# A recorded order of work for a two-layer linear-attention kernel, with its first loads on one queue and more zero matmuls

## The chip, the cores and the metric

The kernel runs on one core of a Trainium2 chip. Five engines work side by side, each through its own list of instructions in order: TensorE (PE: matmuls, with its weight loads shown as PEld), VectorE (DVE), ScalarE (ACT), GpSimd (POOL) and SyncE (SP), which here only issues DMAs. An instruction that waits holds up all that stand behind it on its engine. The metric is the device time of one execution in microseconds (us). A profiled execution gives the trace; its span runs from the first to the last instruction.

## What is computed

The reference applies four residual blocks to `x` of 2048 rows by 512 columns in bfloat16: attention, gated unit, attention, gated unit. Both attentions share one set of weights, and both gated units another.

```python
x = x + _A_ref(_layernorm(x), wqkv, w_phi, wo)            # attention, 32 heads of 16
x = x + _B_ref(_layernorm(x), W_gate, W_up, W_down)       # gated unit, 1376 wide
x = x + _A_ref(_layernorm(x), wqkv, w_phi, wo)
x = x + _B_ref(_layernorm(x), W_gate, W_up, W_down)

def _A_ref(x, wqkv, w_phi, wo):
    q, k, v = split(x @ wqkv)                             # by head
    pq, pk = q @ w_phi, k @ w_phi                         # per head, 16 by 16
    phi_q = concat(softmax(pq), softmax(-pq))             # 32 features per head
    phi_k = concat(softmax(pk), softmax(-pk))
    kv, z = sum_s(phi_k * v), sum_s(phi_k)                # over all 2048 rows
    o = (phi_q @ kv) / (phi_q @ z + 1e-6)
    return o @ wo

def _B_ref(x, W_gate, W_up, W_down):
    gate = x @ W_gate
    return ((gate * (gate > 0)) * (x @ W_up)) @ W_down
```

Because `kv` and `z` are sums over all rows, no row can be attended before the keys of every row are done. This is the one barrier in each layer.

## The kernel before, in words

The rows are cut into 16 tiles of 128 rows, and four tiles make a chunk. `X` stays in the on-chip memory from the first load to the last store; the weights are loaded once.

**Start** (`setup`, `feature_weights`). The projection to keys and `w_phi` are folded into one matrix `Wk2`: TensorE transposes the key weights (L351, 16 matmuls), ACT or DVE copies them out of PSUM (L307, L309), TensorE multiplies by the block matrix `Wblk` that DVE makes of `w_phi` (L327, L364), and ACT casts the result (L307). `Wq2` for the queries is made later in the same way, with DMA transposes (L337). The loads are issued at L225 to L240: the key weights, tiles 1 to 3 of `X` and the value weights on SP; tile 0, `w_phi`, the other tiles and the query weights on ACT. `wake` (L318) multiplies zeros by zeros three times on TensorE, results unused.

**Each layer.** `Norm` takes mean and variance by DVE (L388, L390), the power of minus one half on POOL (L398), scales on ACT (L460) or DVE (L472), and transposes the tile by DMA (L486 for two tiles, L490 for one) or by TensorE (L481). `keys_values` multiplies by `Wk2` (L710), takes both exponentials on ACT (L715), sums them on DVE (L682, or L692 and L688 with a first addition on POOL at L679), inverts (L724), scales on POOL and DVE (L730), multiplies for the values (L663) and adds each tile into `kv` on TensorE (L752). `build_R` turns `kv` into the block matrix `R` (L774, DVE). `queries` does for the queries what was done for the keys (L794, L798, L803, L807, L814), ending in a DMA transpose on SP (L816). `attention` multiplies by `R` (L833), divides (L851, L853), transposes, projects with `wo` (L884) and adds to `X` (L566). `Centre` prepares the gated unit's input (L524, L527, L548, transposes at L535, L539, L542). `glu` runs per chunk, in parts of one to four tiles (`PARTS`): the last 96 columns (L593 to L603), ten gate and ten up products (L613), ReLU and product (L619 to L630), and the down products (L645), added to `X` at L570 or L566. In the second layer, each finished tile goes out by a DMA of SP (L650).

**What sets the order.** No engine's list is written out. Every operation is entered in a `Plan` with an engine, an assumed duration, what it reads and writes, and its buffers. `Plan.order` then plays the program through by these durations: at each moment it takes, for each free engine, the ready operation with the highest rank, which is the length of the chain behind it plus an offset from the table `RANK` for its group and tile. It also picks which of a kind's buffers an operation gets. `emit` writes the operations out in the order so found. `WF_IN` to `X_IN` are the assumed arrival times of the first loads, `LOADED` the time from which the other weights may be loaded. `STEP` chooses, tile by tile, which engine does an operation, how a transpose is done, and how many zero matmuls there are.

Of the kernel before, what the change touches and what calls it, by code (L numbers as in the profile page):

```python
# [8 lines left out]
P = 128  # L9
D = 512  # L10
# [3 lines left out]
NDB = D // P  # L14
# [14 lines left out]
BF16 = mybir.dt.bfloat16  # L29
F32 = mybir.dt.float32  # L30
# [20 lines left out]
TAIL = {"PE": 0.165, "ACT": 0.12, "DVE": 0.115, "POOL": 0.045, "SP": 0.0}  # L51
SAME = {"PE": -0.165, "ACT": 0.035, "DVE": 0.035, "POOL": 0.08, "SP": 0.0}
HOPS = {("DVE", "POOL"): 0.09, ("ACT", "POOL"): 0.15}
NEXT = {"PE": 0.055, "SP": 0.03}
FREE = 0.06


def hop(a, b):
    return SAME[a] if a == b else HOPS.get((a, b), NEXT.get(b, 0.04))


class Plan:
# [10 lines left out]
    def op(self, eng, occ, fn, reads=(), writes=(), holds=(), lat=0.0, at=0.0, group=None, port=False, long=False):  # L73

        o = Op()
        o.eng, o.occ, o.cost, o.fn, o.lat, o.at, o.port, o.long = eng, occ, occ + TAIL[eng], fn, lat, at, port, long
        o.group, o.i_in = group or self.group
        base, slope = RANK.get(f"{o.group}.{eng}") or RANK[o.group]
        o.bias = base - slope * o.i_in
        o.preds, o.succs, o.i = set(), [], len(self.ops)  # L80
        for k in reads:
            w, rs = self.state.setdefault(k, (None, []))
# [16 lines left out]
    def order(self):  # L99
        for o in self.ops:  # L100
            for p in o.preds:
                p.succs.append(o)
        for o in reversed(self.ops):
            o.rank = o.cost + o.lat + max([s.rank + hop(o.eng, s.eng) for s in o.succs], default=0.0)
        free = {k: [0.0] * n for k, (pool, n) in self.kinds.items()}
        engines = sorted({o.eng for o in self.ops})
        busy = {e: 0.0 for e in engines}
        ready = {e: [] for e in engines}
        for o in self.ops:
            o.wait, o.t0 = len(o.preds), o.at  # L110
            if not o.wait:
                ready[o.eng].append(o)
        seq, left, now, shut = [], len(self.ops), 0.0, 0.0
        while left:
            moved, later = False, []
            for e in engines:
                if busy[e] > now + 1e-9:
                    later.append(busy[e])
                    continue
                best = None  # L120
                for o in ready[e]:
                    if o.t0 > now + 1e-9:
                        later.append(o.t0)
                        continue
                    if o.port and shut > now + 1e-9:
                        later.append(shut)
                        continue
                    ok = True
                    need = {}
                    for b in o.bufs:  # L130
                        if b.slot is None:
                            need[b.kind] = need.get(b.kind, 0) + 1
                    for k, n in need.items():
                        got = [t for t in free[k] if t is not None]
                        if len(got) < n:
                            ok = False
                        else:
                            t = sorted(got)[n - 1]
                            if t > now + 1e-9:
                                later.append(t)  # L140
                                ok = False
                    if ok and (best is None or (o.rank + o.bias, -o.i) > (best.rank + best.bias, -best.i)):
                        best = o
                if best is None:
                    continue
                o = best
                ready[e].remove(o)
                moved, left = True, left - 1
                o.start, end = now, now + o.cost
                busy[e] = now + o.occ  # L150
                if o.long:
                    shut = end
                later.append(busy[e])
                for b in o.bufs:
                    if b.slot is None:
                        b.slot = min((i for i, t in enumerate(free[b.kind]) if t is not None),
                                     key=lambda i: free[b.kind][i])
                        free[b.kind][b.slot] = None
                        b.end = 0.0
                    b.left -= 1  # L160
                    b.end = max(b.end, end + o.lat + FREE)
                    if not b.left:
                        free[b.kind][b.slot] = b.end
                for s in o.succs:
                    s.wait -= 1
                    s.t0 = max(s.t0, end + o.lat + hop(e, s.eng))
                    if not s.wait:
                        ready[s.eng].append(s)
                seq.append(o)
            if not moved:  # L170
                later = [t for t in later if t > now + 1e-9]
                assert later, "the plan is stuck"
                now = min(later)
        self.seq = seq
        return seq
# [833 lines left out]
```

## Time and profile before

| | before |
|---|---|
| runs, median (lowest to highest) | 382.15 us (380.12 to 382.57), three runs |
| profiled execution, its own time | 380.91 us |
| its span | 379.2 us |
| TensorE busy | 363.6 us, 96% of the span |
| DVE, ACT, POOL busy | 268.0, 205.5, 121.1 us |
| moved by DMA | 32.61 MB, 8.44 MB of it read from HBM |

The profiled execution took 1.71 us more than its span, and stands 1.24 us below the median of the runs. Busy shares are means over stages with different limits, so they are read stage by stage below. A row of the timeline gives the start, the duration, the engine, the line, the operation, what it writes and reads, how many follow each other, and in brackets the idle time before it with what ended it. The rows of a table by windows give, for a stretch of the span, its length and the busy time of each engine in it.

### The profile page before, as it was taken

How to read it: one execution, taken by the hardware profiler on the slowest of the kernel's cores; microseconds unless marked ns; L12 is line 12 of the kernel's file. 1: busy time of each engine (PE TensorE's matmuls, PEld its weight loads, DVE VectorE, ACT ScalarE, POOL GpSimd, SP SyncE). 2: the span in 40 equal slices, each digit the busy share in tenths (PEclk: the TensorE clock that was granted, in tenths of full speed). 3: DMA queues.
4: the chain of work that ended last, by engine and by line, in shares of the span. 5: the costliest groups of instructions: out<-in, count | busy, mean ns of one | idle time of the engine just before them, and what ended most of it. 6: DMA issues, size and time to landing. Idle time of an engine off the chain costs nothing.

```text
span 379.2 us, 6724 instructions
## 1 busy us (share of the span) xinstructions
PE 363.6 (96%) x2380; PEld 189.9 (50%) x2409; DVE 268.0 (71%) x608; ACT 205.5 (54%) x439; POOL 121.1 (32%) x203
## 2 busy tenths in 40 slices
PE   4898999999899999999999999999999999999996
PEld 2444545756445444444444456475654445454444
DVE  4999999999925442763497998999962675172433
ACT  4898979776762446737706925865234135514100
POOL 3798965131110220560155681724310002000000
PEclk9999999999999999999999999999999999999999
DMA  8889936788950230021013070478930075000011
GB/s 262 239 143 227 260 44 144 133 149 146 145 107 2 42 58 15 0 30 27 0 22 77 9 119 3 87 127 146 171 85 14 5 146 115 14 0 16 1 55 57
DMA packets 98882, 32.61 MB, mean 86 GB/s; under 512 B 90560, under 2 KB 98336, under 8 KB 98848
## 3 DMA queue, kind: packets, MB, share of 16 engines
q1 hardware_dynamic: 97216, 29.93, 39.7%
q10 hardware_dynamic: 1632, 2.24, 1.8%
q8 instruction: 19, 0.31, 0.4%
q14 instruction: 15, 0.12, 0.1%
HBM read 8.44 MB, written 2.10 MB: 28 GB/s over the span
## 4 chain that ended last, share of the span: by engine, by line
PE 64%; DVE 24%; DMA 6%; issue 2%; ACT 1%; POOL 1%; SPq 0%; POOLq 0%; ACTq 0%
PE ps L613 37%; PE ps L645 14%; PE ps L884 5%; DMA b<-b 4%; DVE sk L682 4%; DVE rk L724 3%; DVE bnst L388 3%; PE ps L794 3%; PE ps L593 3%; DVE sk L692 2%; DVE b L730 2%; PE q L833 2%; DMA X<-in_A_x_dram 2%; DVE sq L682 1%; DVE sk L688 1%
## 5 line engine op out<-in xcount | busy, mean ns | idle before, releaser
L613 PE MATMUL ps<-b,wu 128*128 128x512 bf16 (+2 forms) x400 | 79.2, 336 | 0.6 <-DMA b<-b 0.6
L613 PE MATMUL ps<-b,wg 128*128 128x512 bf16 (+2 forms) x400 | 78.6, 336 | 0.0
L645 PE MATMUL ps<-wd,b 128*128 128x512 bf16 (+3 forms) x368 | 78.1, 366 | 0.3
L623 ACT ACTIVATE b<-ps 128x512 bf16<-128x512 f32 (+2 forms) x100 | 50.5, 520 | 39.6 <-PE ps L613 39.1
L626 DVE SCALAR_TENSOR_TENSOR b<-ps,b 128x512 bf16<-128x512 f32 (+2 forms) x60 | 35.1, 598 | 39.9 <-PE ps L613 38.9
L645 PEld LDWEIGHTS <-b 128*128 128x128 bf16 (+1 forms) x374 | 35.3, 98 | 39.1
L613 PEld LDWEIGHTS <-wg 128*128 128x128 bf16 x400 | 36.1, 98 | 33.1
L613 PEld LDWEIGHTS <-wu 128*128 128x128 bf16 x400 | 36.2, 98 | 32.7 <-issue 0.9
L730 POOL TENSOR_TENSOR b<-b,rk 128x1024 bf16<-128x1024 bf16 (+6 forms) x28 | 37.5, 1351 | 9.6 <-DVE rk L724 7.9
L798 ACT ACTIVATE b<-ps 128x512 bf16<-128x512 f32 x64 | 33.0, 638 | 5.7 <-PE ps L794 5.1
L715 ACT ACTIVATE b<-ps 128x512 bf16<-128x512 f32 x64 | 33.7, 628 | 1.3 <-PE ps L710 1.3
L679 POOL TENSOR_TENSOR b<-b 128x256 f32<-128x256 bf16 x30 | 19.7, 670 | 43.9 <-ACT b L715 34.1
L570 DVE SCALAR_TENSOR_TENSOR X<-ps,r,X 128x512 bf16<-128x512 f32 (+2 forms) x26 | 18.2, 701 | 20.2 <-PE ps L645 20.1
L710 PE MATMUL ps<-Wk,b 128*128 128x512 bf16 x123 | 29.4, 379 | 2.0 <-DMA b<-b 1.2
L884 PE MATMUL ps<-wo,b 128*128 128x512 bf16 x118 | 29.7, 379 | 1.5 <-DMA b<-b 0.9
L630 DVE TENSOR_TENSOR b<-b,b 128x512 bf16<-128x512 bf16 (+2 forms) x40 | 13.5, 348 | 24.0 <-ACT b L623 22.3
L552 POOL TENSOR_SCALAR ve<-tot 128x4 f32<-128x4 f32 x8 | 1.9, 233 | 88.8 <-ACT sq L548 88.8
L663 PE MATMUL ps<-wkv,b 128*128 128x512 bf16 x122 | 29.9, 386 | 0.3
L794 PE MATMUL ps<-Wq,b 128*128 128x512 bf16 x126 | 29.5, 379 | 0.1
L548 ACT ACTIVATE sq<-b 128x512 bf16<-128x512 bf16 x32 | 20.1, 627 | 17.4 <-DVE b L527 17.0
L598 ACT CAST ur<-ps 128x192 bf16<-128x192 f32 (+1 forms) x18 | 5.4, 302 | 32.2 <-PE ps L593 32.1
L814 POOL TENSOR_TENSOR b<-b,rq 128x512 bf16<-128x512 bf16 x19 | 20.2, 1061 | 8.4 <-DVE rq L807 6.1
(94 smaller groups left out, 493.7 us busy)
## 6 DMA issues: line engine op xcount, KB each, us to landing
out_dram<-X SPq DMA_DIRECT2D x15, 128.0 KB, 1.8
X<-in_A_x_dram ACTq DMA_DIRECT2D x3, 512.0 KB, 7.2
b<-b SPq DMA_TRANSPOSE x94, 3.2
wg<-in_B_W_gate_dram SPq DMA_DIRECT2D x8, 160.0 KB, 3.2
wu<-in_B_W_up_dram SPq DMA_DIRECT2D x8, 160.0 KB, 4.0
wd<-in_B_W_down_dram SPq DMA_DIRECT2D x5, 256.0 KB, 4.7
wkv<-in_A_wqkv_dram SPq DMA_DIRECT2D x2, 512.0 KB, 7.1
wq<-in_A_wqkv_dram ACTq DMA_DIRECT2D x1, 512.0 KB, 8.3
```

Source lines behind the costliest of these rows:

```text
L613: nc.tensor.matmul(ps[:], lhsT=wt[:, b, f * P:(f + 1) * P], rhs=xnT[:, lo:hi, b, :], start=(b == 0), stop=(b == NDB - 1))
L623: pl.op("ACT", 0.045 + 0.43 * share, lambda ups=ups, ru=ru, sign=1.0 if fuse else -1.0: nc.scalar.activation(out=ru[:], in_=ups[:], func=A ...
L626: pl.op("DVE", 0.06 + 0.548 * share, lambda gps=gps, ru=ru, h=h, cs=cs: nc.vector.scalar_tensor_tensor(out=h[:, cs], in0=gps[:], scalar=0. ...
L645: nc.tensor.matmul(yps[:], lhsT=hs[f][:fsz, ti * P:(ti + 1) * P], rhs=st.wd[:fsz, f, cols], start=(f == 0), stop=(f == NFT - 1))
L663: nc.tensor.matmul(vp[:], lhsT=xnT[:, ti, kb, :], rhs=st.wkv[:, kb, D:2 * D], start=(kb == 0), stop=(kb == NDB - 1))
L710: nc.tensor.matmul(ps[:], lhsT=xnT[:, ti, kb, :], rhs=w(kb), start=(kb == 0), stop=(kb == NDB - 1))
L715: pl.op("ACT", 0.48, lambda s=s, ek=ek, pk=pk: nc.scalar.activation(out=ek[:, :, s, :], in_=pk[:].rearrange("p (j x) -> p j x", j=8), func ...
L730: eng.tensor_tensor(out=phiK[:, lo:hi, :, :].rearrange("p j s (f h) -> p (j s) f h", h=4), in0=ek[:, lo:hi, :, :].rearrange("p j s (f h) - ...
L794: nc.tensor.matmul(pq[:], lhsT=xnT[:, ti, kb, :], rhs=st.Wq2[:, kb, :], start=(kb == 0), stop=(kb == NDB - 1))
L798: pl.op("ACT", 0.48, lambda s=s, eq=eq, pq=pq: nc.scalar.activation(out=eq[:, :, s, :], in_=pq[:].rearrange("p (j x) -> p j x", j=8), func ...
L814: (nc.vector if on_dve else nc.gpsimd).tensor_tensor(out=e, in0=e, in1=rq[:].unsqueeze(2).to_broadcast([P, 8, DH, 4]), op=Alu.mult)
L884: nc.tensor.matmul(yps[:], lhsT=turned(b), rhs=st.wo[:, b, :], start=(b == 0), stop=(b == NDB - 1))
```

## The change: a recorded order, another row of loads, 26 zero matmuls

- `Plan.order` no longer plays anything through. It takes the operations in the order of a table, `ORDER`, of 1867 numbers, and gives each buffer the free slot that was used longest ago. `RANK` and the assumed gaps between engines go.
- The first loads all stand on SP, in one row: tile 0, tile 1, key weights, tiles 2 and 3, value weights, tiles 4 to 7, 8 to 11, query weights, tiles 12 to 15. Only `w_phi` is issued by ACT.
- `wake` enters 26 zero matmuls; `ORDER` says where each stands.
- `STEP` has other choices of engines, of paired transposes, and of parts (`part0` "3111", first chunk in parts of one, one and two tiles, in place of "4111", one and three). `sA` is 0: ahead of the second layer no chunk takes its mean and variance from sums gathered on the way (`add_sums`, L412); all use L388.
- A second way to compute the keys (`raw`) is entered but not used, as `raw` is 0. The assumed durations only document the table now: they no longer act.

```diff
     def order(self):
-        for o in self.ops:
-            for p in o.preds:
-                p.succs.append(o)
...
-                    if ok and (best is None or (o.rank + o.bias, -o.i) > (best.rank + best.bias, -best.i)):
-                        best = o
...
+        owner = {k: [None] * n for k, (pool, n) in self.kinds.items()}
+        last = {k: [-1] * n for k, (pool, n) in self.kinds.items()}
+        assert sorted(ORDER) == list(range(len(self.ops)))
+        self.seq = [self.ops[i] for i in ORDER]
+        for at, o in enumerate(self.seq):
+            o.place = at
+            assert all(hasattr(p, "place") for p in o.preds), "an operation before what it needs"
+            for b in o.bufs:
+                if b.slot is None:
+                    free = [i for i, u in enumerate(owner[b.kind]) if u is None or not u.left]
+                    b.slot = min(free, key=lambda i: last[b.kind][i])
+                    owner[b.kind][b.slot] = b
+            for b in o.bufs:
+                b.left -= 1
+                last[b.kind][b.slot] = at
+        return self.seq
...
+LOAD_SP = ((0, 1), (1, 2), "k", (2, 4), "v", (4, 8), (8, 12), "q", (12, 16))
+LOAD_ACT = ("f",)
...
-    nc.sync.dma_start(out=wkv[:, :, 0:D], in_=wv[:, :, D:2 * D])
-    nc.scalar.dma_start(out=X[:, 0:1, :], in_=xv[:, 0:1, :])
-    nc.scalar.dma_start(out=wf[:], in_=A_w_phi.rearrange("(b j) d f -> (j d) b f", b=NDB, j=8))
-    nc.sync.dma_start(out=X[:, 1:2, :], in_=xv[:, 1:2, :])
-    nc.sync.dma_start(out=X[:, 2:4, :], in_=xv[:, 2:4, :])
-    nc.sync.dma_start(out=wkv[:, :, D:2 * D], in_=wv[:, :, 2 * D:3 * D])
...
+    for what in LOAD_SP:
+        load(nc.sync, what)
+    for what in LOAD_ACT:
+        load(nc.scalar, what)
...
-    nc.scalar.dma_start(out=X[:, 4:8, :], in_=xv[:, 4:8, :])
-    nc.scalar.dma_start(out=X[:, 8:12, :], in_=xv[:, 8:12, :])
-    nc.scalar.dma_start(out=wq[:], in_=wv[:, :, 0:D])
-    nc.scalar.dma_start(out=X[:, 12:16, :], in_=xv[:, 12:16, :])
...
-    "part0": "4111", "part1": "6111", "tB0": "D---", "tB1": "--DA", "tA": "----", "wev": "ADADAAAAADDAAAAA",
-    "xn1": "ADAADDAPDAADDAAA", "turn": "A-AA", "wake": 3, "fuse0": "AFAA", "fuse1": "FFFF", "gate": 1, "sA": 2,
...
+    "raw": 0, "kev": "ADAD", "part0": "3111", "part1": "6111", "tB0": "DA--", "tB1": "-D-A", "tA": "----",
+    "wev": "ADAAAAAADDDAAAAA", "xn1": "ADADDAADDAADAAAA", "turn": "-A--", "wake": 26, "fuse0": "AFAA",
+    "fuse1": "FFFF", "gate": 1, "sA": 0, "xB0": "DAAAADADADDDDDAD", "xB1": "AAAAAAAADDAAAADA",
...
+ORDER = [int(i) for i in """
+142 127 0 1 126 145 132 8 149 9 2 4 3 5 10 11 12 150 133 139 141 125 140 135 138 129 151 155 159 163 131 143 6 156
...
+1866
+""".split()]
```

Counted in the two built programs, the changed one has 23 more zero matmuls of 512 columns and 4 more transposes by matmul on TensorE; 80 gate and up matmuls of 384 columns become 80 of 256 and 80 of 128. The table also moves most operations: in front of the last attention matmul (L833) of the first layer stood 160 gate and up matmuls (L613) and none of the second layer's keys or queries; in the changed order 340 stand there, with 8 of the second layer's key and 8 of its query matmuls.

157 lines of the change are left out of this document (46 added, 111 removed), and 102 rows, old and new, of tables (ORDER, RANK, STEP).

## The prediction, written before the changed kernel ran

> **What bounds the kernel now.** First the page: span and engines. Then a table by windows cut where the work changes: the start, the first layer's keys, its attention, the middle, the second layer's queries and attention, the last gated unit, the end.
>
> ```profile
> span 379.2 us, 6724 instructions
> PE 363.6 (96%) x2380; PEld 189.9 (50%) x2409; DVE 268.0 (71%) x608; ACT 205.5 (54%) x439; POOL 121.1 (32%) x203
> ...
> 0.00:14.00 14.00, 8.17 (x47) 4.77 (x48) 9.18 (x32) 7.47 (x13) 5.78 (x23) 1.00 0.89 281
> 14.00:57.00 43.00, 40.44 (x306) 20.52 (x309) 43.00 (x88) 38.68 (x76) 36.76 (x48) 1.00 0.75 168
> 57.00:100.00 43.00, 42.05 (x390) 26.40 (x395) 42.48 (x120) 31.67 (x84) 11.91 (x19) 1.00 0.79 147
> 100.00:220.00 120.00, 118.52 (x574) 55.59 (x582) 71.89 (x151) 69.66 (x142) 38.40 (x73) 1.00 0.20 37
> 220.00:280.00 60.00, 58.31 (x554) 35.70 (x558) 56.09 (x138) 31.50 (x76) 24.89 (x37) 1.00 0.59 101
> 280.00:360.00 80.00, 79.79 (x420) 38.52 (x423) 39.16 (x75) 26.52 (x53) 3.38 (x5) 1.00 0.21 45
> 360.00:379.20 19.20, 16.27 (x97) 8.44 (x95) 6.17 (x10) 0.00 (x0) 0.00 (x0) 0.99 0.17 56
> ```
>
> TensorE is the bound: after its length each row has TensorE's busy time, and what is missing to the length is all that a reordering can win. That is 5.83 us before 14 us, then 2.56, 0.95, 1.48, 1.69 and 0.21, and 2.93 at the end: 15.65 in all. From 14 to 57 us DVE is busy without a break (43.00 of 43.00), so there two engines are at their limits. The timeline of TensorE shows that the start costs more than its gaps:
>
> ```profile
> 1.24 1.46 PE L318 MATMUL ps<-zero 128*128 128x512 bf16 x3 [1.24 <-DVE zero L234]
> 5.37 1.89 PE L351 MATMUL ps<-ident,wkv 128*128 128x128 bf16 x16 [2.66 <-DMA wkv<-in_A_wqkv_dram]
> 10.04 0.61 PE L364 MATMUL ps<-Wblk,b 128*128 128x128 bf16 x4 [1.93 <-DVE b L309]
> 12.00 1.80 PE L663 MATMUL ps<-wkv,b 128*128 128x512 bf16 x4
> 13.63 1.89 PE L710 MATMUL ps<-Wk,b 128*128 128x512 bf16 x7
> ...
> 66.93 0.67 PE ps L613 x12
> 80.46 1.95 PE ps L613 x12
> 244.22 0.86 PE ps L794 x4
> ```
>
> The last three rows are from the chain that ended last, in order of time. There, four matmuls of 512 columns take 0.86 us, 0.216 each; 128 columns take 0.056 and 384 columns 0.163. At 12.00 four of 512 took 1.80 (about 0.43 each), so TensorE ran at half pace until about 13.6, after 3.6 us of unbroken work from 10.04. The granted clock reads 1.00 throughout and does not show it.
>
> **Part 1, the loads.** Landings from the page, the waits for them, and the bytes by window:
>
> ```profile
> X<-in_A_x_dram ACTq DMA_DIRECT2D x3, 512.0 KB, 7.2
> wkv<-in_A_wqkv_dram SPq DMA_DIRECT2D x2, 512.0 KB, 7.1
> X<-in_A_x_dram SPq DMA_DIRECT2D x1, 256.0 KB, 6.4
> ...
> 6.13 0.42 DVE L327 TENSOR_TENSOR Wblk<-M,wf 128x256 bf16<-128x256 bf16 x1 [1.32 <-DMA wf<-in_A_w_phi_dram]
> 8.25 0.69 DVE L388 BATCH_NORM_STATS2 bnst<-X 128x6 f32<-128x512 bf16 x1 [0.68 <-DMA X<-in_A_x_dram]
> ...
> 0.00:4.00 4.00, 1.46 (x3) 0.29 (x3) 1.18 (x8) 1.49 (x2) 1.32 (x11) 1.00 0.46 116
> 4.00:8.00 4.00, 2.63 (x24) 2.40 (x24) 2.25 (x7) 1.34 (x3) 1.10 (x4) 1.00 1.07 376
> 8.00:12.00 4.00, 2.07 (x17) 1.32 (x15) 3.75 (x12) 2.81 (x6) 2.41 (x7) 1.00 1.08 364
> ```
>
> The last number of a window is GB/s: 0.46 MB are moved by 4 us, 1.97 by 8, 3.42 by 12. The whole set is no smaller afterwards, so its last piece lands when it does now. What changes is who is served first. If one row is served in its order at these rates and a landing follows its last byte by about 0.6 us (my estimate), the key weights (0.79 MB with tiles 0 and 1 ahead) land at 5.5, against TensorE's start on them at 5.37 now; tiles 2 and 3 (1.05 MB) at 6.2 instead of 8.24; the value weights (1.57) at 7.6; tiles 4 to 7 (2.1) at 9.0. `w_phi` no longer has tile 0 ahead of it on ACT, and DVE's wait for it until 6.13 shrinks.
>
> The Trainium skill, "DMA: Bandwidth & Descriptors", section "Issuing engines are not separate DMA queues", says that DMAs of all issuing engines interleave on the same sixteen DMA engines, and that spreading them saves issue time only. By it the order alone can pay, not the number of queues; the unchanged total above agrees.
>
> **Part 2, the first keys.** In the changed order 13 zero matmuls stand ahead of the transposes of the key weights. Starting at 1.24, with 3.6 us at half pace, eight take until 4.8 and five more, at 0.216, until 5.9. That is 0.4 past the landing. The 16 transposes then take 0.9 and end at 6.8 (5.37 plus 1.89 now). ACT afterwards has three copies, a copy of tile 1's transpose and four casts, all in a row:
>
> ```profile
> L307 ACT COPY b<-ps 128x512 bf16<-128x512 bf16 x6 | 3.3, 592 | 2.8 <-PE ps L351 2.8
> L307 ACT CAST Wk<-ps 128x512 bf16<-128x512 f32 x4 | 2.3, 587 | 1.8 <-PE ps L364 1.8
> ```
>
> Four at 0.55 and four at 0.58 are 4.5; from 6.2 (the first four transposes done) this ends at 10.7. The first key matmul follows at about 10.8, at full pace. Now it comes at 13.2, behind the slow value matmuls of 12.00. **Worth 2.4 us there.** Without the full pace it would be some 1 less.
>
> The Trainium skill, "TensorE: Matmul & The Clock Gate", Part 1, states that the array runs at half rate until about 3.4 us of sustained work, and again after an idle window of that length; it calls the whole ramp under 1% of a typical span. The 3.6 us above agree; by 3.4 the zeros end 0.1 earlier.
>
> **Part 3, to the end of the first layer's keys.** Two sums.
>
> ```profile
> 13.20:52.40 39.20, 36.90 (x289) 19.10 (x294) 39.20 (x83) 35.63 (x69) 33.70 (x43) 1.00 0.76 177
> ...
> 50.82 1.01 DVE L730 TENSOR_TENSOR b<-b,rk 128x128 bf16<-128x128 bf16 x2
> ...
> L682 DVE TENSOR_REDUCE sk<-b 128x64 f32<-128x1024 bf16 x14 | 16.5, 1197 | 2.7 <-ACT b L715 2.7
> L388 DVE BATCH_NORM_STATS2 bnst<-X 128x6 f32<-128x512 bf16 x24 | 16.1, 678 | 1.9 <-DMA X<-in_A_x_dram 1.8
> L688 DVE TENSOR_REDUCE sk<-b 128x32 f32<-128x256 f32 x13 | 7.4, 575 | 0.2 <-POOL b L679 0.2
> L309 DVE COPY b<-ps 128x512 bf16<-128x512 bf16 x5 | 2.0, 398 | 0.0
> ```
>
> TensorE, from its first key matmul to the last sum into `kv`: 39.2 us now, 2.3 of it idle. The changed list between the same two points has the same key, value, query and fold matmuls, 8 transposes fewer (−0.45), the two clearing matmuls more (0.24) and 4 zeros (0.86): 39.85, so 10.8 becomes 50.65, 1.75 earlier; were the zeros to stand wholly in present waits, 2.6.
>
> DVE works unbroken from 8.25 to its last key scaling, which ends at 51.83: 43.6 us. In the changed order it has tiles 2 and 3 behind it when tiles 4 to 7 land at 9.0, and from there to the same scaling it has 3 full reductions, 2 statistics, 2 copies, 3 aggregates (0.17) and a scaling (0.44) fewer, 4 half reductions (0.57) and 0.44 of key scaling more: −3.5 −1.4 −0.8 −0.5 −0.4 +2.3 +0.4 = −3.9 in durations, which overlap, so about −3.4 of 43.6. That gives 49.2, 2.6 earlier. **I take 2.2 us, between 0 and 3.5**: 0 if X's later tiles or POOL (which gets 9 instead of 5 early additions for keys) hold DVE up, 3.5 if the waits halve.
>
> **Part 4, work added later.** TensorE has 12 more transposes from here (12 times 0.056, 0.67) and the finer split of the first chunk. A matmul of 256 columns lies between 0.056 and 0.163, middle 0.11; 80 of 0.163 become 80 of 0.11 and 0.056: +0.2. Together **+0.87**, on the bound. On DVE, ACT and POOL the changed assignment adds a few us each to totals far below TensorE's; that is hidden as long as TensorE has other work queued, and part 5 holds what it costs if not.
>
> **Part 5, waits between 57 and 360 us**: 4.33 now. The old order puts all of the first layer's attention against DVE's full stretch to 100 us. The changed one has 340 instead of 160 gate and up matmuls ahead of the last of it, and draws keys and queries of the second layer in front of it, so DVE's work is spread and TensorE has fillers. I take 1.0 off; bounds are 3 off (the windows 57 to 100 and 280 to 360 show that such fillers can leave about 1) and 9 added (rival C). The tail has the same form, 2.93, nothing.
>
> **Sum**: 379.2 − 2.2 + 0.87 − 1.0 = 376.9 us of span, with the 1.71 around it **378.6 us**. Against the profiled execution that is −0.6%, against the median of the runs, 382.15, −0.9%.
>
> **Rivals.**
>
> A. *The waits go.* Part 3 at 3.5 and part 5 at 3 off: 379.2 − 3.5 + 0.87 − 3 + 1.71 = 375.3. For it: all that is needed is that fillers stand at the right places. Against: 96% of the span is work already, and 2.93 us of the rest are the tail.
>
> B. *The start is not handed on.* DVE is the second bound to 57 us; tiles 4 to 7 land later than now (their x3 row is 7.2 from issue, the first of them earlier), POOL adds more, or the zeros end late: at half pace throughout 13 take 5.6 and end at 6.9, a loss of 1.0. Then part 3 is 0 to 0.5 and part 5 is 0: about 381.5. For it: DVE's unbroken row. Against: its list to that point is 3.4 shorter.
>
> C. *SP's list holds the gated unit's weights back*, and it ends slower. SP now issues every weight before the first query transpose.
>
> ```profile
> 52.64 6.47 SPq L816 DMA_TRANSPOSE b<-b  x4
> ...
> wg<-in_B_W_gate_dram SPq DMA_DIRECT2D x8, 160.0 KB, 3.2
> ```
>
> In the changed list the last `wr`, `wu` and `wg` stand behind three query transposes and the last two `wd` behind a fourth, each waiting for POOL's scaling. At the present pace the third is issued near 57, and the weights land near 61. TensorE's first need, now at 66.4 (L593), comes near 62: 2.2 earlier, and 1.8 of query and attention work fewer ahead. So it just fits; with POOL, which scales 14 instead of 8 query tiles, 6 to 9 us late, all TensorE waits, as its list is fixed: 378.6 + 6 to 9, about 386. It decides once the third transpose is issued later than 58.
>
> D. *The table does not hold on the chip.* As an engine never steps past a waiting instruction, small lags add up at many places. The old order is as fixed at run time, so this is no new weakness; it would look like part 5 rising, 380 to 385, and is counted with B.
>
> **Chances.** Forecast 0.43 (376.5 to 380.5), A 0.22, B with D 0.19, C 0.16. Faster by over 1%, below 378.3, is A and half of the forecast: 0.43. Within 1%, about what a measurement can tell here as the three runs before differ by 0.6%: the other half, B, and the mild end of C, 0.42. Slower by over 1%, above 386.0: most of C and a little of D, 0.15. The range holds A down to 373.5 and C to 386.0.
>
> **What would show it.** In the changed profile: the first L351 near 5.9, 16 of them in about 0.9; the first L388 of tile 2 before 7; first key matmul near 10.8 at 0.216; the last L752 of the first layer near 50.2; first L593 near 62 without a DMA wait; TensorE's idle from there to the last glu at about 3.3. A DMA wait at L593, L613 or L645 is C. DVE unbroken with L752 still near 52 is B. I am most likely wrong in part 5, where no row says which instruction will wait.

## The result, and the profile after

The changed kernel is **slower: 392.72 us** (median; 391.39 to 393.77) against 382.36 for the kernel before (median of four runs; the table ahead of the prediction had three of them), a ratio of 1.0277 with a 95% interval of 1.0222 to 1.0333. The forecast of 378.6 us had the wrong sign, and 392.7 lies above the whole range. The profiled execution took 391.39 us, its span is 389.7: 10.5 us more than before. One execution of a later kernel, the run with held loads, took 2210 us and is left out of that run's figures.

The page of the changed kernel (span, engines), then its table by windows with the same cuts:

```profile
span 389.7 us, 6828 instructions
PE 370.3 (95%) x2478; PEld 196.9 (51%) x2516; DVE 284.0 (73%) x619; ACT 202.4 (52%) x450; POOL 128.7 (33%) x202
...
0.00:14.00 14.00, 9.31 (x58) 4.59 (x58) 9.39 (x31) 7.11 (x12) 6.08 (x25) 1.00 0.95 273
14.00:57.00 43.00, 38.20 (x231) 18.17 (x237) 38.19 (x72) 33.25 (x63) 30.79 (x39) 0.92 0.59 141
57.00:100.00 43.00, 38.36 (x417) 25.74 (x422) 42.80 (x109) 29.45 (x87) 23.99 (x38) 1.00 0.57 110
100.00:220.00 120.00, 119.02 (x668) 60.47 (x677) 86.43 (x188) 62.46 (x137) 33.30 (x49) 1.00 0.30 57
220.00:280.00 60.00, 58.94 (x516) 34.16 (x524) 56.38 (x128) 39.86 (x87) 30.73 (x46) 1.00 0.53 85
280.00:360.00 80.00, 79.74 (x454) 40.52 (x459) 39.33 (x81) 28.00 (x63) 3.79 (x6) 1.00 0.30 58
360.00:389.70 29.70, 26.69 (x144) 13.21 (x144) 11.48 (x18) 2.28 (x4) 0.00 (x0) 1.00 0.14 45
```

Three things stand out from 14 to 57 us. TensorE has done 231 matmuls where the kernel before had done 306. DVE, unbroken before, has 4.81 us without work. And the granted clock, the third number from the end, is 0.92.

Windows with fixed cuts hide one thing: where the loss ends. For that, compare one event. Rows of TensorE's timeline, first of the kernel before, then of the changed one (where L752 is L698, L833 is L779, L730 is L676): the last key sums, and the first matmul by `R`, which can only come when all keys are summed.

```profile
52.01 0.41 PE L752 MATMUL q<-vext,b 128*128 128x68 bf16 x8 [0.26 <-ACT vext L307]
...
57.19 0.43 PE L833 MATMUL q<-R,b 128*128 128x68 bf16 x8 [0.45 <-DMA b<-b]
```

```profile
62.04 0.43 PE L698 MATMUL q<-vext,b 128*128 128x68 bf16 x8 [0.83 <-DVE b L676]
...
66.78 0.42 PE L779 MATMUL q<-R,b 128*128 128x68 bf16 x8
```

The latter is 9.59 us later, of 10.5 us in all. From there to the end both take nearly the same, 322.0 us before (379.2 less 57.19) and 322.9 after. So **the loss arises ahead of the first attention**, and what the new order does in the other 83% of the span is as good as the old. TensorE's waits up to 70 us (engine and line that waited, what for; us in total, times, longest):

```profile
PE q L698 <- DVE b L676: 5.6, 5, 2.6
PE ps L593 <- DMA b<-b: 4.0, 1, 4.0
PE ps L248 <- DVE zero L168: 1.2, 1, 1.2
PE ps L281 <- DMA wkv<-in_A_wqkv_dram: 0.6, 1, 0.6
```

The two large ones are new. The second comes first in time; TensorE's timeline, and then the chain of work that ended last, show it:

```profile
1.24 5.18 PE L248 MATMUL ps<-zero 128*128 128x512 bf16 x13 [1.24 <-DVE zero L168]
7.01 1.07 PE L281 MATMUL ps<-ident,wkv 128*128 128x128 bf16 x16 [0.59 <-DMA wkv<-in_A_wqkv_dram]
...
10.54 0.59 PE L248 MATMUL ps<-zero 128*128 128x512 bf16 x2
15.17 1.13 PE L593 MATMUL ps<-wkv,b 128*128 128x512 bf16 x3 [4.03 <-DMA b<-b]
16.09 1.91 PE L640 MATMUL ps<-Wk,b 128*128 128x512 bf16 x4
```

```profile
6.44 8.68 DMA b<-b
15.12 0.05 issue
15.17 0.39 PE ps L593
```

TensorE needs the normalized tile 0, transposed. The change has altered one letter for it: `turn` was "A-AA" and is "-A--". A letter means that TensorE transposes the tile and ScalarE copies it out; "-" means a DMA transpose. Tile 0 now goes by DMA, issued at 6.44 and landed at 15.12, 8.68 us later. And after the idle time the four key matmuls take 1.91 us, where four at full pace take 1.03 (the row at 11.78 of a run below).

The granted clock shows this too, and shows that it happens twice. The longest wait for DVE, 2.61 us, has the same sequel as the wait for the transpose (first TensorE's row, then rows of the table by windows):

```profile
42.49 0.65 PE L698 MATMUL q<-vext,b 128*128 128x68 bf16 x15 [2.61 <-DVE b L676]
```

```profile
14.00:18.00 4.00, 2.78 (x8) 0.93 (x10) 2.73 (x10) 0.59 (x1) 1.37 (x4) 0.75 0.33 66
43.00:47.00 4.00, 3.78 (x22) 1.91 (x20) 4.00 (x8) 2.05 (x4) 3.56 (x3) 0.57 0.83 225
```

The same table cut more finely reads 0.50 from 15.97 to 19.39 us and from 43.28 to 46.70, 3.42 us each time. These two stretches are the 0.92 of the window from 14 to 57 us. So a wait costs more than its own length: half of 3.42 us of TensorE's work comes on top, 1.7 us (an estimate from these two clocks and lengths).

The other large wait is for DVE's part of the key scaling. The two main shapes of that line, before (8.25 to 53.7 us) and after (9 to 67 us; count, busy us, mean ns):

```profile
L730 DVE TENSOR_TENSOR b<-b,rk 128x128 bf16<-128x128 bf16 x6 | 1.5, 274 | 0.0
L730 DVE TENSOR_TENSOR b<-b,rk 128x1024 bf16<-128x1024 bf16 x2 | 1.4, 680 | 0.0
```

```profile
L676 DVE TENSOR_TENSOR b<-b,rk 128x128 bf16<-128x128 bf16 x7 | 6.2, 892 | 0.0
L676 DVE TENSOR_TENSOR b<-b,rk 128x1024 bf16<-128x1024 bf16 x5 | 5.1, 1012 | 0.0
```

The same instruction takes 892 ns in place of 274. The timelines of POOL and of DVE at one such place say why:

```profile
26.91 1.70 POOL L676 TENSOR_TENSOR b<-b,rk 128x896 bf16<-128x896 bf16 x1 [0.68 <-DVE rk L670]
```

```profile
26.75 0.62 DVE L622 TENSOR_REDUCE sk<-b 128x32 f32<-128x512 bf16 x1
27.30 1.39 DVE L676 TENSOR_TENSOR b<-b,rk 128x128 bf16<-128x128 bf16 x1
28.61 0.61 DVE L618 TENSOR_REDUCE sk<-b 128x32 f32<-128x256 f32 x1
```

POOL scales seven blocks of a key tile from 26.91 to 28.61. DVE's scaling of the eighth begins at 27.30 and is over at about the same moment as POOL's. DVE's reduction beside the same POOL instruction, with one input, keeps its 0.62.

Which of the two starts first decides. All five of the slow 128x128 scalings (0.85 to 1.52 us) begin while POOL scales and end within 0.1 us of POOL's end; the other two take 0.15 and 0.21. A 128x1024 scaling that begins just before POOL's is not stretched:

```profile
41.80 0.62 DVE L676 TENSOR_TENSOR b<-b,rk 128x1024 bf16<-128x1024 bf16 x1
```

POOL's scaling begins at 41.96 there, and takes 2.01 us where the one shown above took 1.70. The Trainium skill, "GPSIMD Engine Reference", section "Key points", says that GpSimd shares its SBUF interfaces with VectorE and that they contend when a DVE instruction has two SBUF inputs; the rows agree, and put the price at some 0.6 us on average for an instruction of 0.27.

The planner of the kernel before knew this: at L125 and L126 it does not start an operation marked `port` (DVE's scaling of keys and queries, and some others of DVE with two inputs) while one marked `long` (POOL's scaling or first addition, among others) runs. The recorded order contains no such test, since it is only a list.

Two faults are thus to be told apart: are they two, and are they all?

### The profile page after: what moved, and what is told of

It reads as the page before. It is cut to its first block, busy times and chain, and to the rows that moved or that the text cites. A ratio compares the mean times of both kernels' runs of the same rounds, so it can differ in the third digit from the quotient of the medians.

```text
span 389.7 us, 6828 instructions
## 1 busy us (share of the span) xinstructions
PE 370.3 (95%) x2478; PEld 196.9 (51%) x2516; DVE 284.0 (73%) x619; ACT 202.4 (52%) x450; POOL 128.7 (33%) x202
## 4 chain that ended last, share of the span: by engine, by line
PE 65%; DVE 28%; DMA 3%; issue 2%; ACT 0%; SPq 0%; DVEq 0%
PE ps L543 30%; PE ps L575 18%; PE ps L640 4%; PE ps L830 4%; PE ps L593 4%; DVE sq L622 3%; DVE b L799 3%; DVE b L676 2%; DVE sq L612 2%; PE ps L523 2%; DMA b<-b 2%; DVE sq L618 2%; DVE rk L670 2%; DVE X L496 2%; DVE sq L749 2%
## 5 line engine op out<-in xcount | busy, mean ns | idle before, releaser
L553 ACT ACTIVATE b<-ps 128x512 bf16<-128x512 f32 (+3 forms) x110 | 50.1, 487 | 70.7 <-PE ps L543 65.5
L543 PE MATMUL ps<-b,wu 128*128 128x512 bf16 (+3 forms) x440 | 81.7, 321 | 2.2 <-DVE X L500 0.9
L543 PE MATMUL ps<-b,wg 128*128 128x512 bf16 (+3 forms) x440 | 80.5, 321 | 0.0
L575 PEld LDWEIGHTS <-b 128*128 128x128 bf16 (+1 forms) x374 | 35.5, 98 | 39.2
L676 POOL TENSOR_TENSOR b<-b,rk 128x896 bf16<-128x896 bf16 (+6 forms) x26 | 38.3, 1478 | 26.2 <-DVE b L457 16.6
L500 DVE SCALAR_TENSOR_TENSOR X<-ps,r,X 128x512 bf16<-128x512 f32 (+2 forms) x34 | 23.9, 711 | 30.2 <-PE ps L575 30.0
L661 ACT ACTIVATE b<-ps 128x512 bf16<-128x512 f32 x64 | 36.1, 632 | 15.8 <-PE ps L640 15.8
L744 ACT ACTIVATE b<-ps 128x512 bf16<-128x512 f32 x64 | 34.5, 610 | 10.8 <-PE ps L740 10.7
L593 PE MATMUL ps<-wkv,b 128*128 128x512 bf16 x124 | 32.0, 387 | 4.2 <-DMA b<-b 4.0
L609 POOL TENSOR_TENSOR b<-b 128x256 f32<-128x256 bf16 x37 | 25.3, 698 | 25.6 <-ACT b L661 22.8
L760 POOL TENSOR_TENSOR b<-b,rq 128x512 bf16<-128x512 bf16 x25 | 27.0, 1085 | 2.3 <-DVE rq L753 1.8
L549 ACT ACTIVATE b<-ps 128x128 bf16<-128x128 f32 (+2 forms) x50 | 20.6, 439 | 12.8 <-PE ps L543 12.6
L496 DVE SCALAR_TENSOR_TENSOR X<-ps,X 128x512 bf16<-128x512 f32 x32 | 21.6, 680 | 5.6 <-PE ps L830 5.6
```

The lines of the kernel that those rows point to most:

```text
L496: pl.op("DVE", 0.605, lambda: nc.vector.scalar_tensor_tensor(out=st.X[:, t, :], in0=yps[:], scalar=by() if callable(by) else by, in1=st.X[ ...
L543: nc.tensor.matmul(ps[:], lhsT=wt[:, b, f * P:(f + 1) * P], rhs=xnT[:, lo:hi, b, :], start=(b == 0), stop=(b == NDB - 1))
L553: pl.op("ACT", 0.045 + 0.43 * share, lambda ups=ups, ru=ru, sign=1.0 if fuse else -1.0: nc.scalar.activation(out=ru[:], in_=ups[:], func=A ...
L575: nc.tensor.matmul(yps[:], lhsT=hs[f][:fsz, ti * P:(ti + 1) * P], rhs=st.wd[:fsz, f, cols], start=(f == 0), stop=(f == NFT - 1))
L593: nc.tensor.matmul(vp[:], lhsT=xnT[:, ti, kb, :], rhs=st.wkv[:, kb, D:2 * D], start=(kb == 0), stop=(kb == NDB - 1))
L661: pl.op("ACT", 0.48, lambda s=s, ek=ek, pk=pk: nc.scalar.activation(out=ek[:, :, s, :], in_=pk[:].rearrange("p (j x) -> p j x", j=8), func ...
```

## The experiments

Each ratio is to the kernel before, run beside it on the same chip; that kernel's own median lay between 381.60 and 382.80 us from group to group, so a difference in us between groups carries about 1 us. Line numbers shift by a few lines in the edited kernels. The edits are abridged: `...` or a comment stands for what is left out.

**The loads.** The first suspicion was the row of loads on SP, ahead of the transpose on the same queue. First, the changed kernel with the old issue of loads.

```diff
-LOAD_SP = ((0, 1), (1, 2), "k", (2, 4), "v", (4, 8), (8, 12), "q", (12, 16))
-LOAD_ACT = ("f",)
+LOAD_SP = ("k", (1, 2), (2, 4), "v")
+LOAD_ACT = ((0, 1), "f")
+LOAD_LATER = ((4, 8), (8, 12), "q", (12, 16))      # on ACT, behind the wake activation
```

> The changed kernel with the first loads issued as before (key weights, tiles 1 to 3 and value weights on SP; the rest on ACT); table, zeros and choices stay changed. Theory Q (the loss is the row of loads: DMA transposes on SP's queue stand behind all 3.7 MB of first loads, so tile 0's transpose, issued at 6.44, lands at 15.1): the transposes now stand behind 1.3 MB, land near 12, TensorE's 4.0 us wait halves, 384 to 388 us. Theory T (the recorded order itself loses in the first layer's keys, by DVE and POOL): stays at 390 or more. Theory Z (zeros): no change but for the start, 391 to 393.

391.22 us, ratio 1.0241 [1.0203, 1.0278]: at most a small part of the loss. Tile 0's transpose still took 7.83 us.

Then the row on ACT's queue, so that SP holds nothing ahead of the transpose but `w_phi`:

```diff
+LOAD_SP = ("f",)
+LOAD_ACT = ((0, 1), (1, 2), "k", (2, 4), "v")      # the rest on ACT, behind the wake activation
```

> The changed kernel with the same row of loads on ACT's queue in place of SP's, w_phi on SP; nothing but transposes then stands on SP's queue until the other weights. Theory Q: tile 0's transpose lands about 3 us after its issue, near 10.5, the first key matmul comes near 11, no half clock at 16 to 19 us, and the last sum into kv falls from 62.5 to 51 to 53: 380 to 383 us. Theory T: the transpose lands early but the last sum into kv stays at 58 or later, 388 us or more. Theory Z: as T.

394.98 us, ratio 1.0349 [1.0311, 1.0388]. The chain of waits:

```profile
6.54 10.29 DMA b<-b
16.83 0.05 issue
16.88 0.61 PE ps L596
```

With a queue of SP's that held nothing but `w_phi`, the transpose took 10.29 us. That it stands behind the loads *in SP's queue* is not the reason.

Third, the kernel before with the new row of loads:

```diff
-    nc.sync.dma_start(out=wkv[:, :, 0:D], in_=wv[:, :, D:2 * D])      # and L228 to L240
+    # one row on SP: x tiles 0, 1, key weights, 2-3, value weights, 4-7, 8-11, query weights, 12-15
+    # w_phi alone on ACT
```

> The kernel before with its first loads as in the change (all in one row on SP, w_phi on ACT); its own order, three zeros. Theory Q: its first transposes are issued on SP only near 10.7, when most of the row has passed, so they land near 15 instead of 13.5; it gives back 1 to 3 us: 383 to 386. Theory T and Z: no more than 1 us either way, 381 to 383.5.

380.77 us, ratio 0.9985 [0.9962, 1.0008]: in this kernel the row neither costs nor wins anything that can be measured, and the 1 to 3 us that the suspicion asked for are not there. Fourth, the second of these kernels with only three zeros:

```diff
-  lambda z=z: nc.tensor.matmul(z[:], lhsT=st.zero[:, 0:P], rhs=st.zero[:], start=True, stop=True)
+  lambda z=z, i=i: nc.tensor.matmul(...) if i in (19, 4, 3) else None       # the first three of the order
```

> As the run with the row on ACT's queue, with only the first 3 of the 26 zero matmuls. If the zeros help by keeping TensorE's pace (my step in the prediction): 1 to 2 us slower than that run, first key matmuls at 0.43 us each. If they only take room: 0 to 1.5 us faster, as 13 of them took 5.18 us at half pace and 4 to 6 more stand ahead of work that is ready. Theory Q takes no side.

393.8 us, ratio 1.0317 [1.0289, 1.0345], within the scatter of the run before it: the zeros gain nothing there.

**One fault or two.** The changed kernel with tile 0 turned by TensorE, at the same place of the recorded order:

```diff
-  pl.op("SP", 1.29, lambda xn=xn, ti=ti: nc.sync.dma_start_transpose(out=self.dst[:, ti, :, :], in_=xn[:]),
+  pl.op("SP", 1.29, turn_or_dma,        # tile 0: four transposes by TensorE, copied out by ScalarE
```

> The changed kernel with one edit: key tile 0 is turned by TensorE and copied out by ScalarE at the same place of the recorded order, where the change gives it to a DMA transpose (8.7 us from issue to landing, TensorE's wait for it 4.03 us). Theory 'one late tile': the wait starts everything late, and the later waits (VectorE 4.8 us, TensorE 5.6 us behind VectorE's scaling of keys, the clock of .5 after the idle) follow from it; then 382 us or less, ratio 0.99 to 1.00. Theory 'two faults': the scaling that VectorE and GpSimd do at the same time (892 ns an instruction where the kernel before has 274) is built into the recorded order, and stays; then 386 to 388 us, ratio 1.010 to 1.018, with VectorE's 128x128 scaling still over 700 ns.

388.73 us, ratio 1.0152 [1.0094, 1.0211]. The 4.0 us wait is gone, as these waits up to 70 us show, and the other stands as before:

```profile
PE q L707 <- DVE b L685: 5.6, 5, 2.6
PE ps L248 <- DVE zero L168: 1.2, 1, 1.2
PE ps L281 <- DMA wkv<-in_A_wqkv_dram: 0.8, 1, 0.8
```

DVE's 128x128 scaling still takes 891 ns. "Two faults" holds: the collision does not follow from the late tile. Now the collision alone, POOL's scaling cut to one block:

```diff
-  lambda scale=scale, cut=cut: scale(nc.gpsimd, 0, cut)
+  lambda scale=scale: scale(nc.gpsimd, 0, 1)         # sums(): src = 0 if j < cut else j
```

> The changed kernel, with GpSimd's part of the key scaling cut to its first block (the sums over keys use that block for all blocks of GpSimd's part, so this work is left out of the computation). Theory 'the collision costs': VectorE's scaling goes back to about 274 ns for 128x128 and 680 for 128x1024, the 5.6 us that TensorE waits for it go, and the time falls by 5 to 7 us to 386 to 388. Theory 'one late tile': the scaling only fills time in which TensorE waits anyway for the late tile; the time falls by 2 us or less. To be read against the same cut in the kernel before.

384.76 us, ratio 1.0059 [1.0033, 1.0085], 8.0 us less than the changed kernel and more than either theory had; DVE's groups by shape:

```profile
L676 DVE TENSOR_TENSOR b<-b,rk 128x1024 bf16<-128x1024 bf16 x5 | 3.8, 762 | 0.0
L676 DVE TENSOR_TENSOR b<-b,rk 128x128 bf16<-128x128 bf16 x7 | 1.6, 231 | 0.0
```

This cut also removes work of POOL's, so the kernel before was cut by the same two lines (its L736 and L752):

> The kernel before with the same cut of GpSimd's scaling to one block (that work is left out of the computation): the control. Its order keeps VectorE's scaling out of GpSimd's long operations, so both theories expect little: 0 to 2 us less, 379.5 to 381.6 us. More than 3 us less would say that GpSimd's share bounds both kernels, and that the comparison with the changed one says nothing of a collision.

381.03 us, ratio 0.9955 [0.9932, 0.9979]. The work left out is worth 1.7 us there, so some 6 of the 8 us belong to the changed order alone: to the collision, or to the length of POOL's scaling in it. A run further down tells these two apart. And the kernel before with tile 0 turned by DMA:

```diff
+  if self.at and t == 0:     # the same places in the plan, no transposes by TensorE, and in place of the copy:
+      nc.sync.dma_start_transpose(out=self.dst[:, ti, :, :], in_=xn[:])
```

> The kernel before with one part of the change alone: key tile 0 is turned by a DMA transpose in place of TensorE and ScalarE, the order of the other operations nearly as before. Theory 'one late tile': the transpose lands only when the loads end, near 14 us where the first keys could begin at about 12, and the time grows by 3 to 6 us, to 385 to 388. Theory 'two faults' too expects a loss, but 1 to 3 us, since the planner of the kernel before does not start VectorE's scaling beside GpSimd's whatever comes late. No loss would mean that tile 0's way is not the cause at all.

386.47 us, ratio 1.0089 [1.0054, 1.0124]: 3.4 us lost by this alone, with a wait of 3.4 us for the transpose. The size is near the 4.0 us that the opposite edit won, but the way is another. Here SP issues tile 0's transpose only at 12.46, behind tile 1's, and it lands 2.9 us later. So the run shows that tile 0 by DMA costs this kernel too; it does not show a transpose held up by loads.

**Are they all.** Both edits together in the changed kernel (of POOL's scaling only one block is left, as above):

> The changed kernel with both edits: tile 0 turned by TensorE, and GpSimd's key scaling cut to one block (that work is left out of the computation). Theory 'two faults': the late tile (4.0 us by its own run) and the collision (8.0 us by its own run) are separate and together all of the loss; 380 to 382 us, level with the kernel before under the same cut (381.0). Theory 'the table holds more': something else in the recorded order costs too, and 3 us or more are left over the kernel before under the same cut: 384 us or more.

380.1 us, ratio 0.9941 [0.9924, 0.9958], level with the kernel before under the same cut (0.9955). "Two faults" holds: with POOL's scaling out of the way, no third one of a size that can be measured is left. Next the planner's rule, in the kernel before:

```diff
-                    if o.port and shut > now + 1e-9:
+                    if False:
```

> The kernel before with one line of its planner taken out: the rule by which VectorE's two-input operations are not started while a long GpSimd operation runs. Theory 'collision': the planner, free of it, puts such pairs side by side, VectorE's 128x128 scaling of keys goes from 274 ns to 500 or more, and the time grows by 1 to 5 us (383.5 to 388). Theory 'table': the stretching comes of where the recorded order happens to put things, and this kernel stays within 1 us of 382.8 because its first stage is bound by TensorE anyway.

393.48 us, ratio 1.0286 [1.0253, 1.032]. DVE's groups up to 67 us:

```profile
L730 DVE TENSOR_TENSOR b<-b,rk 128x128 bf16<-128x128 bf16 x6 | 4.9, 819 | 0.0
L730 DVE TENSOR_TENSOR b<-b,rk 128x1024 bf16<-128x1024 bf16 x2 | 2.4, 1194 | 0.0
```

Without the rule the planner puts the pairs side by side, and the stretching appears in the kernel before too. More was lost than expected, and not all of it by the collisions: of 13.2 us of span, 5.6 are lost up to the first matmul by `R` (62.77) and the rest later, in an order that is new everywhere. What cost that rest was not traced.

Then a mending that keeps the computation: where POOL scales seven blocks and DVE the eighth, POOL scales all eight. With tile 0 turned by TensorE:

```diff
-  lambda scale=scale, cut=cut: scale(nc.gpsimd, 0, cut)
+  lambda scale=scale, cut=cut: scale(nc.gpsimd, 0, 8 if cut == 7 else cut)
-  lambda scale=scale, cut=cut: scale(nc.vector, cut, 8)
+  lambda scale=scale, cut=cut: None if cut == 7 else scale(nc.vector, cut, 8)
```

> The changed kernel with tile 0 turned by TensorE, and, where GpSimd scales seven of a key tile's eight blocks and VectorE the eighth, GpSimd scales all eight (the same computation, 0.2 us more of GpSimd each, one VectorE instruction of 892 ns less each). Theory 'collision': VectorE only sits out GpSimd's operation in these, so some 6 us of VectorE come free in the first 62 us, and most of it is seen: 383 to 386 us against 388.7 with tile 0 alone. Theory 'share of work': it is GpSimd's own length that holds TensorE; then 388 to 390 us.

383.45 us, ratio 1.0035 [1.0017, 1.0053]. More work for POOL and less for DVE wins 5.3 us between the medians (3.5 between the profiled spans): what cost in these scalings was DVE's sitting out, not POOL's length. The rows of the two runs from the first key matmul to the last key sum show how it reached TensorE, first with tile 0 alone, then this run:

```profile
12.57:57.42 44.85, 38.95 (x287) 19.58 (x291) 44.85 (x82) 36.54 (x69) 35.58 (x46) 0.96 0.62 141
12.39:54.30 41.91, 37.17 (x287) 19.14 (x291) 41.90 (x74) 36.33 (x69) 37.25 (x46) 1.00 0.66 152
```

Of 2.94 us, TensorE's waits are 1.16. The other 1.78 is busy time, for the same 287 matmuls: the longest wait for DVE, 2.62 us with half pace after it, became 1.99 us, and no half pace followed. Last of this group, the loads in one row and 13 zeros in place of 3 ahead of the key weights in the kernel before:

```diff
-  lambda z=z: nc.tensor.matmul(z[:], ...)
+  zeros                                  # the third of three emits eleven, so 13 in all
```

> The kernel before with two parts of the change that are not the table: the loads in one row, and 13 zero products in place of 3 ahead of the first weights. If full pace for the 16 turns of the key weights (1.07 us in the changed kernel, 1.89 here with 3 zeros) is handed on to the first keys, the time falls by about 1 us to 379.5 to 381.5; if the first keys wait for tile 1's DMA transpose and for the copies of the weights anyway, nothing: 380.5 to 382.

381.54 us, ratio 0.9985 [0.997, 0.9999]: both parts together win at most 0.3%, at the edge of what these runs can tell from no change.

**What held the transpose.** The changed kernel with its last three loads (1.5 MB) issued behind tile 0's transpose:

```diff
-LOAD_SP = ((0, 1), (1, 2), "k", (2, 4), "v", (4, 8), (8, 12), "q", (12, 16))
+LOAD_SP = ((0, 1), (1, 2), "k", (2, 4), "v", (4, 8))
+LOAD_HELD = ((8, 12), "q", (12, 16))                 # issued right behind tile 0's transpose
```

> The changed kernel with its last three loads (x tiles 8 to 11, the query weights, x tiles 12 to 15; 1.5 MB) issued behind tile 0's DMA transpose on SyncE's queue, in place of ahead of it. Theory 'loads in flight': the transpose lands when what was issued before it has been moved, so by 11 us in place of 15.1; TensorE's wait of 4.0 us for it goes or is under 1 us, and the time falls by 2 to 4 us to 388.5 to 390.5 (388.7 with TensorE turning tile 0). Theory 'a first transpose is slow': it still takes some 8 us from issue to landing whatever is in flight, and the time stays at 391.5 to 394.

388.49 us (median of three; 388.37 to 392.35), ratio 1.0182 [1.0115, 1.0248], an interval that still touches the changed kernel's; the profiled execution took 388.37 us, against 391.39. The time alone does not settle it, the landing does. TensorE's timeline:

```profile
10.39 0.59 PE L250 MATMUL ps<-zero 128*128 128x512 bf16 x2
10.91 1.04 PE L599 MATMUL ps<-wkv,b 128*128 128x512 bf16 x3
11.78 1.03 PE L646 MATMUL ps<-Wk,b 128*128 128x512 bf16 x4
...
17.95 1.04 PE L646 MATMUL ps<-Wk,b 128*128 128x512 bf16 x4 [2.11 <-DMA b<-b]
```

The transpose was issued at 6.47, and its reader starts at 10.91 without a wait: at most 4.4 us in place of 8.7. So a DMA transpose waits for the loads in flight when it is issued. Its landing follows that of the last load issued ahead of it: 10.9 after 10.4 us here, 15.1 after 14.6 in the changed kernel, 14.6 after 14.2 with the old loads, and 16.83 after 16.76 with the row on ACT, where the loads stood on another queue. The next transposes, now behind the held loads, come late in their turn (2.11 us). The Trainium skill, "DMA: Bandwidth & Descriptors", section "Issuing engines are not separate DMA queues", says that DMAs from all issuing engines share the same sixteen DMA engines and interleave there. The run with the row on ACT agrees in that a queue of its own did not help; that the transpose then came behind the whole row is what the runs add.

The kernel before with the loads in one row and all four first tiles turned by TensorE:

```diff
-    "turn": "A-AA",
+    "turn": "AAAA",
```

> The kernel before with the loads in one row and with all four tiles of the first norm turned by TensorE (tile 1 by a DMA transpose so far, for which TensorE waits 1.2 us at 14.9 us); the planner orders the work anew. Theory 'loads in flight': the wait for tile 1 goes and the first keys follow one another; 379 to 381 us. Theory 'TensorE is what bounds': four more turns and a copy on ScalarE take what the wait gave; 380.8 to 382.5.

392.93 us, ratio 1.0273 [1.022, 1.0326]; both theories missed. The planner made a new order of it, in which the first key matmul comes at 16.6 in place of 13.2, behind the values of four tiles. The first matmul by `R` comes at 60.65, so 3.5 of 12.3 us of span are lost ahead of it and the rest later. DVE's 128x128 scaling takes 229 ns there, so this loss is of another kind; it was not traced further. It says how far one letter moves a planned order, and limits what can be read from the run without the rule.

Last, the mended kernel with two of DVE's remaining collisions moved (key tiles 1 and 6):

```diff
+        for o, n in self.later:           # DVE's scaling of the two tiles, n = 2
+            # o is put behind the next n operations of DVE in the recorded order
```

> The changed kernel with tile 0 turned by TensorE and GpSimd scaling all eight blocks where it scaled seven (383.45 us), and VectorE's scaling of key tiles 1 and 6 put two VectorE instructions later in the recorded order, out of GpSimd's scaling of another tile (2.05 and 1.79 us there, where the kernel before takes 0.67). Theory 'collision': 1 to 2.5 us less, 381 to 382.5 us, level with the kernel before. If the time stays at 383 to 384, what is left of the collisions lies off the path.

383.61 us, ratio 1.0038 [1.0015, 1.0061]: nothing. The five whole-tile scalings still take 1456 ns on average (1598 without the move). In the mended kernel TensorE still waits 4.5 us for DVE's scaling, and 1.5 us in the run with both edits, where POOL's is cut. Whether the 0.35% that is left comes from there stays open. No version that does the whole computation was faster than the kernel before by an amount that counts.

The first matmul by `R` puts the main runs on one scale, since what follows it takes 322 to 323.4 us in each of them:

| kernel | first matmul by `R`, us | ratio |
|---|---|---|
| before | 57.19 | 1 |
| changed | 66.78 | 1.0277 |
| changed, tile 0 by TensorE | 61.74 | 1.0152 |
| the same, POOL scales eight | 58.62 | 1.0035 |
| before, tile 0 by DMA | 61.10 | 1.0089 |

Of 9.59 us, 5.04 are the late tile and 3.12 the split scaling, each with the half pace that came after its wait; 1.43 are left.

## Why the prediction was wrong

**What bounds.** Right, and it misled. "What is missing to the length is all that a reordering can win" said nothing of what a reordering can lose.

**Part 1, the loads.** Right in part, and the worth nothing. DVE makes its block matrix from `w_phi` without a wait, as forecast. But the key weights land at 7.0 (TensorE waits for them and starts at 7.01), not at 5.5; tiles 2 and 3 land at 7.8, not 6.2; tiles 4 to 7 at 10.4, not 9.0. My estimate of a row served in its order at full rate was 1.4 to 1.6 us too early, and no row was given for the 0.6 us between last byte and landing that went into it. The kernel before with this row is level with itself.

**Part 2, the first keys: the step that failed.** "From 6.2 [...] this ends at 10.7. The first key matmul follows at about 10.8, at full pace." ScalarE's row ended at about 11.7, which is an error of 1, the one of part 1: the weights came later. But the first key matmul came at 16.1: I followed the key *weights* and not the *tile* that they are multiplied with. The diff shows `turn`, and part 3 even counted the transposes that TensorE loses. It did not ask where they go, nor when a DMA transpose lands that is issued at 6.4 amid loads that run to 14. That a transfer can wait for those ahead of it was in part 1, applied to loads alone. Worth +2.9 in place of −2.4 there.

The zeros: 13 took 5.18 us and ended at 6.42, not 5.9. I had eight at half pace and five at full; ten went at half pace, and the last three, from 5.48 on, took 0.94 us, where the first two had taken 1.03. So full pace came at about 5.7, 4.5 us after the first zero. The 16 transposes behind them then took 1.07, full pace as forecast. The gain was lost anyway when TensorE idled for 4.03 us and fell back to half pace. By the Trainium skill's 3.4 us ("TensorE: Matmul & The Clock Gate", Part 1) full pace would have come at 4.6; it came about 1 us later.

**Part 3, to the last key.** TensorE's sum of 39.85 us became 46.4 (16.1 to 62.47), against 39.2 before. Of the 7.2 us more, TensorE's idle time is 3.7 (6.0 in place of 2.3) and its busy time 3.5, which is mostly the two stretches at half pace. DVE's sum was made with the durations of the kernel before: "0.44 of key scaling more". The scaling measured 12.0 us where those durations give 5.6 (seven by 0.274, five by 0.680, one by some 0.3). The mis-sized term is a duration that holds only as long as POOL is still. It stood in the code that the change removes: the diff cuts `order`, and with it the test on `shut`. I read it as "plays the program through by these durations" and priced only its result.

**Parts 4 and 5.** From the last key sum to the end both kernels take the same: 327.2 us after (62.47 to 389.7), 326.8 before (52.42 to 379.2). In these stretches TensorE is busy for 319.3 us before and 319.7 after, and idle for 7.5 in both: the work added is nearer +0.4 than +0.87, and the 1.0 off the waits did not come. What I called the weakest part missed by half a microsecond.

**The rivals.** A is out. C did not happen, though its condition did: the third query transpose was issued after 64.9, not 58, but TensorE's first need came at 74.9, not 62, and it has no DMA wait at the gated unit's lines in the first layer. B named the right place ("the start is not handed on"; tiles 4 to 7 did land later, and the zeros did end late), but it priced the late zeros at 1.0 us, where the first key matmul came 2.9 later, and it named neither cause. D's reason for a low chance, "the old order is as fixed at run time, so this is no new weakness", was the mistake: the old order had been made under a rule.

**What would show it.** First L351 near 5.9: 7.01. First L388 of tile 2 before 7: 8.01. First keys near 10.8 at full pace: 16.1, at half pace. Last L752 near 50.2: 62.47. First L593 near 62 without a DMA wait: 74.9, without one. The first wrong row of the list already stands at 7 us.

## What to carry to other kernels

When a planner is replaced by its own kind of output, read what its rules forbade: each rule is a cost that the list must avoid by itself. For a step that moves from a compute engine to a DMA, price the landing by when the last load ahead of it lands, not by its median row (3.2 us here, 8.7 amid the first loads). A wait of TensorE that is followed by half pace is to be priced with that pace (an estimated 1.7 us each time here). And durations of two-input DVE instructions are to be taken from a place where POOL does the same thing as in the plan.

## What was not expected of the hardware

- A DMA transpose of one tile took 8.68 us from issue to landing amid the first loads, and 10.29 on a queue of its own; with the last 1.5 MB held back, at most 4.4. In four runs it landed 0.1 to 0.5 us after the last load issued ahead of it.
- DVE's two-input scaling of one block, when it begins while POOL scales, lasts until POOL's instruction ends: 274 ns on average in the kernel before, 892 in the changed one, 231 with POOL's cut short. Begun before POOL's, a scaling of a whole tile took 0.62 us, not longer.
- TensorE went at half pace for the first 4.5 us of zeros, and again for 3.42 us after an idle time of 4.03 us and after one of 2.61; the granted clock of the last two stretches reads 0.50. After an idle time of 1.99 us, in the mended kernel, it stayed at 1.00.
